# Issuing the first weight quarter and the last row tile's stores from a second engine's DMA queue

## The chip, the cores and the metric

The kernel runs on one core of one Trainium2 chip. The metric is the device time of one execution in microseconds (us). A run also leaves a span (first to last instruction, about 1.7 us shorter than the time) and the mean clock that TensorE was granted, as a share of full speed. Executions are compared on the same chip; those of other chips are only set beside them.

Names: PE is TensorE, PEld its weight loads, DVE VectorE, ACT ScalarE, SP SyncE. SPq and ACTq are the instruction queues of SyncE and ScalarE, from which DMAs are issued. L156 is line 156 of the kernel file; the change adds one line near the top, so L156 of before is L157 of after.

## The reference

The reference mixes two attention blocks over the same input with a gate. Cut to what matters:

```python
x = A_x                                             # [1, 2048, 1024] bf16
g = sigmoid((x * gate_w).sum(-1, keepdims=True))
a = linear_attention(x, A_wqkv, A_wo)               # pq, pk = phi(q), phi(k); 32 heads of 32
b = local_attention(x, B_wqkv, B_wo)                # window 8, dilation 2
return g * a + (1 - g) * b
```

The part that the change touches is the first product of block A: pk = phi(x @ Wk), with x transposed on its way in and Wk of 1024 x 1024.

## The kernel before

All loads go through SyncE's queue, in this order. A "row tile" is 128 rows of x; each is transposed by the DMA (crossbar transpose) into xT. The first half of Wk (512 columns) comes as four quarters, the second half as one load of 1 MB.

```python
WkA = [wpool.tile([P, KT, 512], BF16, name="WkA0", tag="wa")]
nc.sync.dma_start_transpose(out=xT[:, :, 0:P], in_=rows(x, 0, P))
for i in range(4):
    if i == 2:
        nc.sync.dma_start_transpose(out=xT[:, :, P:2 * P], in_=rows(x, P, 2 * P))
    nc.sync.dma_start(out=WkA[0][:, 2 * i:2 * i + 2, :],
                      in_=A_wqkv[2 * i * P:(2 * i + 2) * P, D:D + 512].rearrange("(kt p) n -> p kt n", p=P))
for t in range(2, NB):
    nc.sync.dma_start_transpose(out=xT[:, :, t * P:(t + 1) * P], in_=rows(x, t * P, (t + 1) * P))
WkA += load_w("WkA", A_wqkv, D, "wa", only=(1,))    # the second half of Wk
# ... cut: rows of x, other weights
```

TensorE runs in program order. It starts with 36 small warm-up matmuls, then row tiles 0 and 1 together, as the weight quarters arrive (`kt` 0 to 3 needs quarters 1 and 2), then tiles 2 to 15 for the first half of the columns, then all tiles for the second half.

```python
warm_up(36)
first = [ps_1.tile([P, 512], F32, name="pk_ps", tag="p1") for _ in range(2)]
for t, kts in ((0, (0, 1, 2, 3)), (1, (0, 1, 2, 3)), (0, (4, 5)), (1, (4, 5)), (0, (6, 7)), (1, (6, 7))):
    for kt in kts:
        project(first[t], t, kt, 0)
    # ... cut: phi when a tile is complete
for half in range(2):
    for t in range(NB):
        # ... cut: skips tiles 0 and 1 in half 0
        for kt in range(KT):
            project(pj, t, kt, half)
        phi(pk[:, t, half * 512:(half + 1) * 512], pj)
# ... cut: 350 us of other stages
# in the last stage, for every row tile tb:
nc.scalar.activation(out=osb[:, 0:n], in_=st["ps"][:, 0:n], func=ACT.Copy, scale=omg[:, tb:tb + 1])
nc.sync.dma_start(out=rows(out2, tb * P, (tb + 1) * P)[:, c0:c0 + n], in_=osb[:, 0:n])
```

The softmax here doesn't subtract the row's maximum and nothing guards it: scores larger than these inputs give would overflow.

## Time and profile before

| | before |
|---|---|
| first three runs | 491.37, 491.40, 491.46 us |
| profiled run | 492.63 us: span 490.9 us, mean clock 0.995 |
| PE busy | 484.8 us, 99% of the span |
| unbroken PE work starts | 7.99 us |
| half-clock stretch | 8.41 to 11.82 us (from the clock records) |

The first view is the page of the kernel before: the span, PE's busy time, the granted clock in 40 slices, and the chain that ended last by engine.

```profile
span 490.9 us, 8143 instructions
PE 484.8 (99%) x3332; PEld 230.5 (47%) x3332; DVE 279.1 (57%) x512; ACT 188.4 (38%) x283; POOL 16.0 (3%) x33
...
PEclk8999999999999999999999999999999999999999
...
PE 98%; DMA 1%; SPq 0%; ACT 0%; issue 0%; ACTq 0%
```

PE is the bound, so a few us at the two ends are all that is left outside it. The digit 8 in the first slice (12 us wide) says that PE did not have its full clock there. The clock records begin only at 4.99 us; before that the warm-up matmuls start 0.107 us apart, about twice the 0.056 us of the same matmuls at full clock, so PE had half its clock there too.

The chain that ended last, in order of time, over the first 25 us of before: start, duration, what.

```profile
0.80 1.33 SPq L95
2.13 0.06 issue
2.19 0.57 SPq L99
2.76 0.05 issue
2.81 0.46 SPq L99
3.26 0.04 issue
3.31 4.64 DMA xT<-in_A_x_dram
7.95 0.04 issue
7.99 17.18 PE pk_ps L156 x71
```

SyncE issues one DMA after the other: the first transpose (L95), two weight quarters (L99), the second transpose. PE's unbroken run begins when that transpose has landed. Each issue ahead of it is on the chain, and the first quarter's place is 0.57 + 0.05 us.

The same stretch by windows, before: window, its length, busy time of each engine (and instructions), then the granted clock, the busy share of the DMA engines and GB/s.

```profile
5.00:8.00 3.00, 1.32 (x7) 0.30 (x4) 0.00 (x0) 0.00 (x0) 0.00 (x0) 1.00 1.08 264
8.00:12.00 4.00, 4.00 (x11) 1.51 (x12) 0.00 (x0) 0.00 (x0) 3.16 (x15) 0.57 1.10 252
34.00:36.00 2.00, 2.00 (x11) 0.88 (x9) 1.37 (x3) 0.60 (x1) 0.00 (x0) 1.00 1.05 387
```

From 5 to 8 us PE works 1.32 of 3 us. From 8 to 12 us it is busy all the time but does only about 10 matmuls, where 4 us at full clock hold 18: the clock is 0.57. The DMA engines are busy throughout (shares over 1 are overlapping packets).

### The profile page before, as it was taken

To read this page: it belongs to the slowest core of one execution; us is meant where nothing else is said; L and a number is where in the kernel's file an instruction comes from. 1 tells how busy PE (TensorE), PEld (TensorE's weight loads), DVE (VectorE), ACT (ScalarE), POOL (GpSimd) and SP (SyncE) were. 2 spreads that over 40 slices of the span, in tenths; PEclk is the share of its full clock that TensorE was granted. 3 is DMA by queue.
4 is the path that set the end of the run, shared out by engine and by line. 5 is a ranking of instruction groups with operands and counts; after the bars stand their busy time and mean duration, and the time that the engine had idled before them with its cause. 6 is when DMAs were issued, how large, how long until landed. Compare 5 with 4: busy or idle time off the path is not lost.

```text
span 490.9 us, 8143 instructions
## 1 busy us (share of the span) xinstructions
PE 484.8 (99%) x3332; PEld 230.5 (47%) x3332; DVE 279.1 (57%) x512; ACT 188.4 (38%) x283; POOL 16.0 (3%) x33
## 2 busy tenths in 40 slices
PE   7999999999999999999999999999999999999997
PEld 4444444446444444444445444445545444444444
DVE  0766689993328999997366666656655596000000
ACT  1333311111443333332566665666664332212121
POOL 3000000402000000000000000000000000000000
PEclk8999999999999999999999999999999999999999
DMA  8999960000621222236011151111163953111111
GB/s 193 153 276 371 348 224 0 0 1 5 216 62 61 91 95 88 63 125 196 3 30 37 32 115 30 30 36 29 37 151 81 212 87 85 33 43 33 43 34 43
DMA packets 80181, 46.56 MB, mean 95 GB/s; under 512 B 53520, under 2 KB 74128, under 8 KB 80144
## 3 DMA queue, kind: packets, MB, share of 16 engines
q1 hardware_dynamic: 80144, 46.04, 35.4%
q8 instruction: 26, 0.43, 0.4%
q14 instruction: 11, 0.09, 0.1%
HBM read 21.23 MB, written 7.34 MB: 58 GB/s over the span
## 4 chain that ended last, share of the span: by engine, by line
PE 98%; DMA 1%; SPq 0%; ACT 0%; issue 0%; ACTq 0%
PE kq_ps L331 23%; PE d_ps L444 21%; PE pk_ps L156 11%; PE g_ps L204 11%; PE p_ps L254 11%; PE p_ps L288 8%; PE q_ps L288 3%; PE oB L382 3%; PE s L357 2%; PE q_ps L444 1%; DMA xT<-in_A_x_dram 1%; PE kv_ps L220 1%; PE p_ps L243 1%; SPq L95 0%; SPq L99 0%; ACT osb L449 0%
## 5 line engine op out<-in xcount | busy, mean ns | idle before, releaser
L367 ACT ACTIVATE PT<-s 128x896 bf16<-128x896 f32 (+1 forms) x72 | 63.0, 926 | 24.5 <-PE s L357 24.5
L331 PE MATMUL kq_ps<-xT,WkB 128*128 128x512 bf16 x256 | 65.3, 379 | 0.0
L331 PE MATMUL kq_ps<-xT,WqB 128*128 128x512 bf16 x256 | 64.8, 379 | 0.0
L368 DVE TENSOR_TENSOR PT<-PT,mask 128x896 bf16<-128x896 bf16 (+1 forms) x72 | 44.7, 624 | 26.6 <-ACT PT L367 26.5
L156 PE MATMUL pk_ps<-WkA,xT 128*128 128x512 bf16 x256 | 57.4, 387 | 1.7 <-DMA WkA<-in_A_wqkv_dram 0.9
L254 PE MATMUL p_ps<-WvB,xT 128*128 128x512 bf16 x256 | 58.5, 379 | 0.0
L444 PE MATMUL d_ps<-WoA,pqT 128*128 128x512 bf16 (+1 forms) x248 | 56.9, 372 | 0.0
L444 PE MATMUL d_ps<-WoB,OBT 128*128 128x512 bf16 (+1 forms) x248 | 56.9, 372 | 0.0
L204 PE MATMUL g_ps<-pk,xrow 128*128 128x512 bf16 x256 | 55.4, 379 | 0.0
L144 DVE TENSOR_SCALAR e<-e 128x512 f32<-128x512 f32 x64 | 27.2, 425 | 43.5 <-ACT e L143 43.5
L449 ACT ACTIVATE osb<-d_ps,omg 128x512 bf16<-128x512 f32 (+1 forms) x31 | 20.9, 674 | 76.2 <-PE d_ps L444 76.1
L288 PE MATMUL p_ps<-WqA,xT 128*128 128x512 bf16 x192 | 43.4, 379 | 0.0
L156 PEld LDWEIGHTS <-xT 128*128 128x128 bf16 x256 | 25.5, 100 | 33.5 <-issue 3.5
L336 ACT CAST kqt<-kq_ps 128x512 bf16<-128x512 f32 x48 | 28.2, 588 | 31.8 <-PE kq_ps L331 31.6
L444 PEld LDWEIGHTS <-pqT 128*128 128x128 bf16 x264 | 25.8, 98 | 29.5
L444 PEld LDWEIGHTS <-OBT 128*128 128x128 bf16 x264 | 25.8, 98 | 29.3
L204 PEld LDWEIGHTS <-xrow 128*128 128x128 bf16 x256 | 25.0, 98 | 30.2
L254 PEld LDWEIGHTS <-xT 128*128 128x128 bf16 x256 | 25.0, 98 | 30.0
L288 PEld LDWEIGHTS <-xT 128*128 128x128 bf16 x256 | 24.3, 98 | 28.5
L143 ACT ACTIVATE e<-pk_ps 128x512 f32<-128x512 f32 x32 | 19.0, 597 | 43.8 <-PE pk_ps L156 43.8
L331 PEld LDWEIGHTS <-WqB 128*128 128x128 bf16 x256 | 23.0, 97 | 24.7
L331 PEld LDWEIGHTS <-WkB 128*128 128x128 bf16 x256 | 22.6, 97 | 24.1
(57 smaller groups left out, 400.3 us busy)
## 6 DMA issues: line engine op xcount, KB each, us to landing
xrow<-in_A_x_dram SPq DMA_DIRECT2D x4, 1024.0 KB, 12.7
out_dram<-osb SPq DMA_DIRECT2D x31, 128.0 KB, 1.9
pqd<-tmp SPq DMA_DIRECT2D x12, 256.0 KB, 2.1
WvA<-in_A_wqkv_dram SPq DMA_DIRECT2D x2, 1024.0 KB, 16.6
WoA<-in_A_wo_dram SPq DMA_DIRECT2D x2, 1024.0 KB, 13.7
WvB<-in_B_wqkv_dram SPq DMA_DIRECT2D x2, 1024.0 KB, 11.9
WqA<-in_A_wqkv_dram SPq DMA_DIRECT2D x2, 1024.0 KB, 10.0
WkB<-in_B_wqkv_dram SPq DMA_DIRECT2D x2, 1024.0 KB, 7.4
```

What stands on the lines that cost most here:

```text
L143: nc.scalar.activation(out=e[:], in_=pj[:], func=ACT.Exp)
L144: nc.vector.tensor_scalar(out=e[:], in0=e[:], scalar1=1.0, scalar2=1e-6, op0=ALU.min, op1=ALU.add)
L156: nc.tensor.matmul(pj[:], lhsT=xT[:, kt, t * P:(t + 1) * P], rhs=WkA[half][:, kt, :], start=(kt == 0), stop=(kt == KT - 1))
L204: nc.tensor.matmul(pj[:], lhsT=xrow[:, t, kt * P:(kt + 1) * P], rhs=pk[:, t, half * 512:(half + 1) * 512], start=(t == 0), stop=(t == NB - 1))
L254: nc.tensor.matmul(st["pj"][:], lhsT=xT[:, kt, t * P:(t + 1) * P], rhs=WvB[half][:, kt, :], start=(kt == 0), stop=(kt == KT - 1))
L288: nc.tensor.matmul(st["pj"][:], lhsT=xT[:, kt, t * P:(t + 1) * P], rhs=WqA[half][:, kt, :], start=(kt == 0), stop=(kt == KT - 1))
L331: nc.tensor.matmul(st["pj"][:], lhsT=W[c // 4][:, kt, (c % 4) * P:(c % 4 + 1) * P], rhs=xT[:, kt, cols], start=(kt == 0), stop=(kt == KT - 1))
L336: (nc.vector.tensor_copy if 0 <= after < 4 else nc.scalar.copy)(out=kqt[:, which, cols], in_=st["pj"][:])
L367: nc.scalar.activation(out=ptv[:, hs], in_=s4[:, hs, 0:W_], func=ACT.Exp, scale=SCALE)
L368: nc.vector.tensor_tensor(out=ptv[:, hs], in0=ptv[:, hs], in1=m[:, None, :].broadcast_to([P, 2, W_]), op=ALU.mult)
L444: nc.tensor.matmul(st["ps"][:, 0:n], lhsT=lhsT, rhs=W[c0 // 512][:, c, c0 % 512:c0 % 512 + n], start=(side == 0 and c == 0), stop=(side == ...
L449: nc.scalar.activation(out=osb[:, 0:n], in_=st["ps"][:, 0:n], func=ACT.Copy, scale=omg[:, tb:tb + 1])
```

## The change

The intent: SyncE's queue gives up one slot at the start, so that everything behind it goes out earlier, and the quarter itself leaves beside the first transpose. At the end, ScalarE, which evicts the last results, also stores them, without handing over to SyncE.

```diff
     for i in range(4):
         if i == 2:
             nc.sync.dma_start_transpose(out=xT[:, :, P:2 * P], in_=rows(x, P, 2 * P))
-        nc.sync.dma_start(out=WkA[0][:, 2 * i:2 * i + 2, :],
-                          in_=A_wqkv[2 * i * P:(2 * i + 2) * P, D:D + 512].rearrange("(kt p) n -> p kt n", p=P))
+        (nc.sync if i else nc.scalar).dma_start(
+            out=WkA[0][:, 2 * i:2 * i + 2, :],
+            in_=A_wqkv[2 * i * P:(2 * i + 2) * P, D:D + 512].rearrange("(kt p) n -> p kt n", p=P))
# ... cut
-                    nc.sync.dma_start(out=rows(out2, tb * P, (tb + 1) * P)[:, c0:c0 + n], in_=osb[:, 0:n])
+                    (nc.sync if tb < NB - 1 else nc.scalar).dma_start(
+                        out=rows(out2, tb * P, (tb + 1) * P)[:, c0:c0 + n], in_=osb[:, 0:n])
```

## The prediction

> **What bounds it now.** TensorE. The page gives PE 484.8 us busy of a 490.9 us span (99%), and the chain of waits is 98% PE. The change touches only the two ends.
>
> *Start* (chain of waits and timeline, 0 to 20 us). SyncE issues one after the other: first transpose 0.80, 1.33 us long; weight quarter at 2.19 (0.57 us); second quarter 2.81 (0.46); second transpose 3.31 (1.25), which lands 4.64 us after its start. PE runs 36 warm-up matmuls from 1.12 to 5.13, then waits 0.69 and 0.22 us for the first two weight quarters and 0.76 us for the second transpose. From 7.99 on PE never waits again in this stage.
>
> There is also a clock effect. The records show full clock from 4.99 to 8.41 us, half clock from 8.41 to 11.82 (3.41 us), then full. In that stretch matmuls start every 0.43 us instead of 0.216, so about 1.7 us of PE work is lost. The window before it, 4.99 to 8.41, was about 37% busy (four matmuls and 0.4 us).
>
> *End.* Last matmul ends 487.6; the last eviction takes 0.475 us to 488.18; SyncE issues the last store at 488.21 (0.33 us); it lands about 1.6 us later; the rest is barrier.
>
> **What the change does.** The first quarter's issue leaves SyncE's queue; the order listing puts it on ScalarE directly behind the 1.28 us table load (0.79 to 2.07), with no wait. Every later SyncE issue moves up one slot: 0.57 + 0.05 = about 0.62 us. The second transpose should start near 2.7 and land near 7.3. The quarter itself goes at about 0.9, if the table load does not hold ScalarE's sequencer, or at about 2.1; both are early enough, since PE is in its warm-up until 5 us. So PE's unbroken run starts about 0.6 us sooner, and all 0.6 us is on the chain.
>
> Can later loads keep up? Transposes land at least 1.66 us before PE needs them; the second half of the weights lands 35.88, and is used from 36.45: 0.57 us of slack, and it moves earlier too. So 0.6 us survives; a gain much over 1.2 us would be cut there.
>
> The end: the same hop (0.03 us) and the same issue time, on another engine. Only three stores move, and ScalarE is idle over 1 us before each last eviction, so a 0.33 us issue does not delay it. I expect 0 ± 0.1 us.
>
> **Against the gain.** The Trainium skill, "Perfetto Trace Analysis", DMA Instruction — HWDGE, says that the descriptor generator is locked for exclusive use and that the profiled window includes the wait for that lock. If so, the two issues serialise and the gain is nil. No trace of one queue shows it. "DMA: Bandwidth & Descriptors", Issuing engines are not separate DMA queues, says a second engine saves only the sequencer's issue time: my 0.6 us.
>
> **For more.** If the earlier start makes the 4.99 to 8.41 window busy enough (about 55%), the half-clock stretch could vanish, for up to 0.6 us more before the weight slack binds. I give it one in four.
>
> **Prediction:** 490.8 us, range 489.9 to 491.5. Faster by over 2%: 0.01; within 2%: 0.98; slower: 0.01.
>
> **Right if** the second transpose is issued near 2.7 us and not longer than 1.3 us; the quarter's issue on ScalarE overlaps the first transpose; PE's run starts near 7.4; the span from the last matmul to the end is unchanged at 3.3 us.
>
> **Wrong if** the issues of the two queues lengthen each other; the early quarter delays the first transpose's data; the half-clock window moves or vanishes; or ScalarE's issue is slower and delays the end.

## The result, and the profile after

| | before | after |
|---|---|---|
| median | 491.38 us (6 runs) | 490.98 us (6 runs) |
| lowest to highest | 490.72 to 492.78 | 490.68 to 491.80 |
| profiled run | span 490.9, clock 0.995 | span 489.7, clock 0.999 |

The ratio of after to before is 0.9992, with a 95% interval of 0.9976 to 1.0007. A ratio here is the mean time of one kernel's fast runs over that of the other's of the same rounds, so not quite the ratio of the medians quoted. The two samples overlap, and the first three runs of before, within 0.09 us of each other, had hidden a spread of 2 us.

The page of after:

```profile
span 489.7 us, 8140 instructions
PE 483.1 (99%) x3332; PEld 229.5 (47%) x3332; DVE 279.1 (57%) x512; ACT 188.0 (38%) x283; POOL 16.3 (3%) x33
...
PEclk9999999999999999999999999999999999999999
...
PE 92%; SPq 5%; DMA 2%; issue 0%; ACT 0%
```

The clock digit 8 is gone, PE's busy time is 1.7 us less for the same 3332 matmuls, and the chain now has 5% of SyncE's queue in it. The timeline of after, 0 to 12 us (start, duration, engine, line, operation, what; in brackets the idle time before it and its end), shows the issues and the matmuls:

```profile
0.79 1.28 ACT L70 ACT_TABLE_LOAD   x1 [0.79 <-PEq L495]
...
0.80 1.34 SPq L95 DMA_TRANSPOSE xT<-in_A_x_dram  x1
0.83 0.44 ACTq L99 DMA_DIRECT2D WkA<-in_A_wqkv_dram  x1
...
2.20 0.56 SPq L99 DMA_DIRECT2D WkA<-in_A_wqkv_dram  x1
2.82 1.25 SPq L98 DMA_TRANSPOSE xT<-in_A_x_dram  x1
...
6.13 0.59 PE L157 MATMUL pk_ps<-WkA,xT 128*128 128x512 bf16 x2 [0.87 <-DMA WkA<-in_A_wqkv_dram]
...
7.26 1.04 PE L157 MATMUL pk_ps<-WkA,xT 128*128 128x512 bf16 x4 [0.54 <-DMA xT<-in_A_x_dram]
8.53 3.83 PE L157 MATMUL pk_ps<-WkA,xT 128*128 128x512 bf16 x17 [0.23 <-DMA WkA<-in_A_wqkv_dram]
```

The quarter goes out at 0.83 us, while the table load runs on ScalarE and SyncE issues the transpose. Neither issue is longer than it was on SyncE's queue alone (1.34 against 1.33 us; 0.44 against 0.57). The second transpose is issued at 2.82 in place of 3.31, and tile 1 starts at 7.26 in place of 7.99.

Then come waits that before's profile did not have: one at 8.53 for the third weight quarter, and one near 35 us. The windows of after, and the chain that ended last from 25 to 40 us:

```profile
5.00:8.00 3.00, 1.58 (x8) 0.48 (x6) 0.00 (x0) 0.00 (x0) 0.00 (x0) 1.00 1.12 250
8.00:12.00 4.00, 3.77 (x19) 1.52 (x18) 1.31 (x3) 1.09 (x2) 3.00 (x14) 1.00 1.11 210
34.00:36.00 2.00, 1.48 (x8) 0.51 (x6) 1.36 (x4) 0.60 (x1) 0.00 (x0) 1.00 1.04 399
```

```profile
27.05 8.11 DMA WkA<-in_A_wqkv_dram
35.16 0.05 issue
35.21 4.92 PE pk_ps L157 x22
```

With the full clock, PE reached the second half of Wk before it had landed (35.16 us) and waited 0.68 us: that is where the chain goes over to SyncE's queue. In before, PE came to this point at 36.45, after the landing (35.88).

From there on the two programs are equal. The time from the first matmul of the second half to the last matmul of the kernel is 450.90 us in before and 450.91 in after. So the whole difference of the two spans (1.24 us) is made in the first 36 us: 36.45 against 35.21. The profiles of the experiments below say the same, where their matmul records are complete: the span less the start of the second half is 454.4 or 454.5 us in all of them, and 454.3 where that half comes in four loads (e7, e8, e9).

The end of before, and the end of after:

```profile
487.71 0.47 ACT L449 ACTIVATE osb<-d_ps,omg 128x256 bf16<-128x256 f32 x1 [1.27 <-PE d_ps L444]
488.21 0.33 SPq L451 DMA_DIRECT2D out_dram<-osb  x1
```

```profile
486.43 0.47 ACT L450 ACTIVATE osb<-d_ps,omg 128x256 bf16<-128x256 f32 x1 [1.27 <-PE d_ps L445]
486.93 0.34 ACTq L452 DMA_DIRECT2D out_dram<-osb  x1
```

Eviction start to store issue is 0.50 us in both; from the start of the last matmul to the start of the last instruction it is 3.51 and 3.50 us.

The question left by the result: is the half-clock stretch part of the old start, or did it fall by chance on one profile and not on the other? And how much of 1.24 us comes from the freed slot?

### The profile page after: what moved, and what is told of

It reads as the page before. It is cut to its first block, busy times and chain, and to the rows that moved or that the text cites. A ratio compares the mean times of both kernels' runs of the same rounds, so it can differ in the third digit from the quotient of the medians.

```text
span 489.7 us, 8140 instructions
## 1 busy us (share of the span) xinstructions
PE 483.1 (99%) x3332; PEld 229.5 (47%) x3332; DVE 279.1 (57%) x512; ACT 188.0 (38%) x283; POOL 16.3 (3%) x33
## 4 chain that ended last, share of the span: by engine, by line
PE 92%; SPq 5%; DMA 2%; issue 0%; ACT 0%
PE kq_ps L332 23%; PE d_ps L445 21%; PE g_ps L205 11%; PE p_ps L255 11%; PE p_ps L289 8%; PE pk_ps L157 6%; SPq L103 4%; PE q_ps L289 3%; PE oB L383 3%; PE s L358 2%; DMA WkA<-in_A_wqkv_dram 2%; PE q_ps L445 1%; PE kv_ps L221 1%; PE p_ps L244 1%; SPq L99 0%; SPq L95 0%
## 5 line engine op out<-in xcount | busy, mean ns | idle before, releaser
L157 PE MATMUL pk_ps<-WkA,xT 128*128 128x512 bf16 x256 | 56.2, 379 | 2.2 <-DMA WkA<-in_A_wqkv_dram 1.6
```

Of the source, the lines that this page charges most:

```text
L157: nc.tensor.matmul(pj[:], lhsT=xT[:, kt, t * P:(t + 1) * P], rhs=WkA[half][:, kt, :], start=(kt == 0), stop=(kt == KT - 1))
```

## The experiments

Theory A: the first quarter's move does two things. It frees a slot (earlier transposes), and it makes PE less idle around 5 to 8 us, so that the clock is not halved afterwards. Rival B: the half clock comes by chance with the phase of a free-running window, whatever the kernel, and the gain is that chance. Rival C: the stores carry the gain.

Each experiment has six runs (the profiled one and five timed). Below, spans are sorted and "low" marks a mean clock of 0.997 or less (one stretch of 3.41 us at half clock takes 0.0035 from the mean of a 490 us span). A "long" run is one of 490.0 us span or more. The four kernels of a group ran on one chip, beside 11 runs of the kernel before. The first six runs of the changed kernel, of the result above, had spans of 489.0, 489.0, 489.0, 489.4, 489.7 and 490.1 us, none low.

### Group 1: repeats, and the two halves of the change apart

**b1_before_again** is the kernel before, unchanged.

> The kernel before, unchanged, to see its spread of span and clock run by run. Theory A (the half-clock stretch is part of the old start): most runs show a mean clock near 0.995 and spans near 490.9 us. Rival B (the stretch comes and goes with the phase of the clock window, whatever the kernel): some runs show 0.995 and some 0.999, and those at 0.999 are 0.5 to 0.6 us shorter, not 1.7 us, because the second half of the weights lands at 35.9 us and cuts the rest.

**b1_after_again** is the changed kernel, unchanged.

> The changed kernel, unchanged. Theory A: every run near clock 0.999 or above, spans 489.0 to 490.1 us as in its first six runs, and the spread comes from the landing of the second half of the weights (35.2 us in its first profile), so that the start of the next PE tile follows that landing. Rival B: some runs at 0.995, with spans of 490.2 us or more.

**e1_quarter_only** undoes the second part of the change:

```diff
-                    (nc.sync if tb < NB - 1 else nc.scalar).dma_start(
-                        out=rows(out2, tb * P, (tb + 1) * P)[:, c0:c0 + n], in_=osb[:, 0:n])
+                    nc.sync.dma_start(out=rows(out2, tb * P, (tb + 1) * P)[:, c0:c0 + n], in_=osb[:, 0:n])
```

> Only the first weight quarter moves to ScalarE's queue; all stores stay on SyncE. If the start carries the whole effect: same as the changed kernel within 0.2 us (about 491.0 us, ratio 0.999), second transpose issued near 2.8 us. If the stores carry it: as before, 491.4 us.

**e2_stores_only** is the kernel before with the second part alone:

```diff
-                    nc.sync.dma_start(out=rows(out2, tb * P, (tb + 1) * P)[:, c0:c0 + n], in_=osb[:, 0:n])
+                    (nc.sync if tb < NB - 1 else nc.scalar).dma_start(
+                        out=rows(out2, tb * P, (tb + 1) * P)[:, c0:c0 + n], in_=osb[:, 0:n])
```

> Only the stores of the last row tile move to ScalarE's queue; the quarter stays on SyncE. Expected: no gain, ratio 1.000 within 0.001, and last matmul to end of span 3.50 us as in both profiles (3.51 before, 3.50 after). If the stores carry the effect: 0.4 us faster than before.

Spans of the runs (us):

```
before (11)      488.9 489.0 489.0 489.0 489.1 489.4 | 490.6 490.6low 490.9low 491.0low 491.0low
b1_before_again  489.0 489.1 489.1 489.4 489.4       | 491.4low
e2_stores_only   489.1 489.1 489.1 489.3             | 490.4 491.1low
b1_after_again   488.4 488.6 488.6 488.7 489.1 489.5
e1_quarter_only  488.1 488.6 488.9 489.0 489.0 489.3
```

Ratios to before: 0.9995 (b1_before_again, 0.9974 to 1.0017), 0.9981 (b1_after_again, 0.9962 to 1.0000), 0.9980 (e1_quarter_only, 0.9962 to 0.9999), 1.0000 (e2_stores_only, 0.9976 to 1.0023).

The kernel before has two kinds of runs: around 489.1 us, and around 490.9 us, the latter mostly with a low clock. So the profile that the prediction was made from was of the rarer kind, and theory A as first written for the repeat ("most runs near 0.995") is wrong. Rival B's numbers for before fit better, but not its core: a low clock did not come "whatever the kernel". It came in 6 of 23 runs with the old start and in none of 12 with the quarter on ScalarE. Rival C falls: the stores alone give 1.0000, and the quarter alone gives as much as both. In e2's profile the time from the start of the last matmul to that of the last instruction is again 3.50 us. The repeat of the changed kernel came out shorter than expected (488.4 to 489.5 us).

The profile of b1_before_again, at full clock, is the fair partner of after. Its windows:

```profile
5.00:8.00 3.00, 1.53 (x7) 0.48 (x6) 0.00 (x0) 0.00 (x0) 0.00 (x0) 1.00 1.10 277
8.00:12.00 4.00, 4.00 (x19) 1.60 (x18) 1.18 (x1) 1.08 (x2) 3.51 (x18) 1.00 1.13 228
```

From 8 to 12 us PE works on 19 matmuls at a clock of 1.00, as many as in after: what before's profile lost there was the clock.

At full clock, too, the new start is faster: 488.8 us on average (b1_after_again) against 489.1 in the 11 short runs of before and its repeat (group 3 puts this in doubt).

### Group 2: fill the idle time, keep the slot, move more

**e3_before_fill** lets PE do small matmuls of no use while it waits for the second transpose; no load moves.

```diff
+            warm = ps_1.tile([P, P], F32, name="warm", tag="p1")
             def warm_up(n):
-                warm = ps_1.tile([P, P], F32, name="warm", tag="p1")
# ... cut
             for t, kts in ((0, (0, 1, 2, 3)), (1, (0, 1, 2, 3)), (0, (4, 5)), (1, (4, 5)), (0, (6, 7)), (1, (6, 7))):
+                if t == 1 and kts[0] == 0:
+                    warm_up(16)
                 for kt in kts:
```

> The kernel before with 16 more idle-filling matmuls (about 0.9 us at full clock) where TensorE waits for the second transpose; no load is moved. Theory A (the half-clock stretch follows from too little matmul work in one clock window: 1.3 us of work in the window that was followed by the stretch, about 1.6 us in one that was not): no run with a clock of 0.997 or less, all spans 488.9 to 489.5 us, so faster on average than before by about 0.1 to 0.2% but no faster than the full-clock runs of before. Rival (the stretch is chance, unrelated to that idle time): slow runs of 490.4 to 491.4 us in about a third of the runs, as before.

**e4_slot_kept** puts a tiny load, which nobody reads, into the freed place of the changed kernel.

```diff
+        if i == 0:
+            slot = wpool.tile([P, 2, 16], BF16, name="slot", tag="slot", bufs=1)
+            nc.sync.dma_start(out=slot[:], in_=A_wo[0:2 * P, 0:16].rearrange("(kt p) n -> p kt n", p=P))
         (nc.sync if i else nc.scalar).dma_start(
```

> The changed kernel with a tiny transfer (8 KB, same count of rows) put into the place on SyncE's queue that the first quarter left. Theory A (the gain is the freed issue slot): second transpose issued near 3.3 us again, TensorE's unbroken run starts 0.4 to 0.6 us later than in the changed kernel, full-clock spans back at about 489.1 us. Rival (the gain is the early landing of the first quarter, 3.7 instead of 5.8 us): spans stay at 488.6 us.

**e5_act_all** moves all four quarters.

```diff
-        (nc.sync if i else nc.scalar).dma_start(
+        nc.scalar.dma_start(
```

> All four quarters of the first weight half on ScalarE's queue, SyncE issues only transposes. Slot theory carried on: second transpose issued near 2.2 us, third near 3.5, one more slot each; TensorE's run starts near 6.4 us and the span falls by up to 0.6 us more, to 488.0. If the DMA engines are the limit by now (busy share about 1.1 from 5 to 12 us): transposes land no earlier than in the changed kernel and the span stays within 0.2 us of 488.6.

**e6_after_fill_split** is the changed kernel with 12 filling matmuls (edit as in e3) and the second half of Wk in four loads:

```diff
-    WkA += load_w("WkA", A_wqkv, D, "wa", only=(1,))
+    WkA.append(wpool.tile([P, KT, 512], BF16, name="WkA1", tag="wa"))
+    for i in range(4):
+        nc.sync.dma_start(
+            out=WkA[1][:, 2 * i:2 * i + 2, :],
+            in_=A_wqkv[2 * i * P:(2 * i + 2) * P, D + 512:D + 1024].rearrange("(kt p) n -> p kt n", p=P))
```

> The changed kernel with 12 idle-filling matmuls before the second row tile, and the second weight half loaded in four quarters instead of one load. The fill can only remove slow runs, which the changed kernel did not show in 12 runs; the split removes the 0.68 us wait for the second half where it occurs (seen in one profile of four). Expected: spans 488.4 to 488.8 us, less spread than the changed kernel's 488.4 to 489.5.

Spans (us), on another chip than group 1:

```
before (11)          489.1 489.2 489.3 489.5 489.8 | 490.0 490.6low 490.8 490.8low 490.9low 491.3low
e3_before_fill       489.2 489.2 489.4 489.5       | 490.2 490.5
e4_slot_kept         489.2 489.3 489.4 489.5 489.7 489.9
e5_act_all           489.2 489.3                   | 490.2 490.4 490.8low 490.9low
e6_after_fill_split  488.7 488.7 488.8 488.9 489.1 489.2
```

Ratios: 0.9990 (e3, 0.9972 to 1.0008), 0.9986 (e4, 0.9971 to 1.0001), 0.9999 (e5, 0.9981 to 1.0016), 0.9973 (e6, 0.9959 to 0.9988).

*e3.* No low clock, as theory A expected, but two long runs with a recorded clock of 1.0, which it did not expect. Only half a hit; the next group goes on from here. By length alone (two long runs of six) the fill is not shown to help; the case for it rests on the recorded clock.

*e4.* The timeline of e4_slot_kept shows SyncE's old times again with the quarter still early:

```profile
0.83 0.45 ACTq L102 DMA_DIRECT2D WkA<-in_A_wqkv_dram  x1
...
2.21 0.56 SPq L101 DMA_DIRECT2D slot<-in_A_wo_dram  x1
2.81 0.46 SPq L102 DMA_DIRECT2D WkA<-in_A_wqkv_dram  x1
3.32 1.25 SPq L98 DMA_TRANSPOSE xT<-in_A_x_dram  x1
...
7.29 1.04 PE L160 MATMUL pk_ps<-WkA,xT 128*128 128x512 bf16 x4 [0.25 <-DMA xT<-in_A_x_dram]
8.73 3.55 PE L160 MATMUL pk_ps<-WkA,xT 128*128 128x512 bf16 x14 [0.41 <-DMA WkA<-in_A_wqkv_dram]
```

The span is what the slot theory expected (mean 489.5, as the short runs of before, 489.4), but the way there is not. The second transpose was issued 0.50 us later than in the changed kernel, and tile 1 still started at 7.29, as good as 7.26: from issue to landing it took 3.9 us in place of 4.4 (4.6 in before). So this landing did not hang on the freed slot: with the quarter early, the second transpose lands at 6.87 to 7.46 us in seven profiles, e4's 7.24 among them, and with the old start at 7.54 to 8.01 in six. The slot seems to be lost further on: in e4's profile the third quarter landed at 8.69 us and the third and fifth row tiles at 10.56 and 13.94, against 8.26, 10.25 and 13.77 in e6, which has the changed kernel's issues and ran on the same chip. That is one profile each, and e9's (8.61, 10.35 and 13.98, with the slot free) is close to e4's, so this is not shown. And e4 had no long run. This suggests, without showing it, that two effects come apart: the quarter's early landing (3.73 us) goes with the missing long runs, the freed slot with about 0.4 us at full clock (489.50 on average against 488.90 in e6, of which about 0.15 belongs to e6's end, as told below). Three cautions: the tiny load has 256 rows of 32 bytes to move, so part of this cost may be its own; e6 has a fill and a split besides the slot; and at the old start's rate of low runs, six without one would come by chance once in 9.

*e5.* The timeline and a window of e5_act_all:

```profile
0.83 6.09 ACTq L99 DMA_DIRECT2D WkA<-in_A_wqkv_dram  x4
2.19 1.69 SPq L98 DMA_TRANSPOSE xT<-in_A_x_dram  x1
6.57 1.04 PE L157 MATMUL pk_ps<-WkA,xT 128*128 128x512 bf16 x4 [1.73 <-DMA xT<-in_A_x_dram]
8.14 4.05 PE L157 MATMUL pk_ps<-WkA,xT 128*128 128x512 bf16 x10 [0.53 <-DMA xT<-in_A_x_dram]
```

```profile
8.00:12.00 4.00, 3.81 (x10) 1.46 (x12) 0.00 (x0) 0.00 (x0) 1.68 (x9) 0.60 1.21 240
```

More of the same change loses everything. The second transpose goes out at 2.19 as planned, but with three quarters issued from ScalarE by 2.3 us the *first* transpose lands at 6.52 us, in place of 4.60 with one quarter beside it and 4.21 with none. PE stands idle for 1.73 us, and the half clock is back (0.60), in two runs of six. Neither expected span came (488.0, or within 0.2 us of 488.6): it is 490.1 us on average, as before's. That the transposes land no earlier did come true (the second at 8.09). The Trainium skill, "DMA: Bandwidth & Descriptors", Queues, rings and completion order, says that each DMA engine takes turns between the queues it has work for; the later landing of the transpose agrees with that. (The fourth quarter waited for a completion semaphore, that of the first transpose, and went at 6.54, so this is not a clean test of all four. The second transpose's issue took 1.69 us here in place of 1.25; why is open.)

### Group 3: the two causes of long runs apart

**e7_before_split** is the kernel before with the split of e6 alone.

> The kernel before with the second weight half loaded in four quarters. Two causes of long runs are supposed: (1) a half-clock stretch after a clock window with under about 40% of matmul work (33% and 37% were followed by one, 42% and more were not), (2) a late landing of the second weight half (35.9 us in the first profile; the span is then that landing plus about 454.4 us). The split takes away only cause 2: long runs (490.0 us and more; 14 of 34 so far with the old start) should become fewer but stay, those that stay showing 0.997 or 0.995 where the clock was recorded. If cause 2 were all: none left.

**e8_before_fill_split** is the kernel before with the fill of e3 and the split.

> The kernel before with the 16 filling matmuls and the split, so with both supposed causes of long runs removed and every issue where it was before. Expected: no run of 490.0 us or more, spans 489.0 to 489.6 us. If long runs remain, there is a third cause. What is then left between this and the changed kernel with fill and split (488.7 to 489.2 us) is the freed issue slot: about 0.3 us.

**e9_after_split** is the changed kernel with the split alone.

> The changed kernel with the split alone. If the changed start itself prevents the half-clock stretch (windows of 47% and more in its profiles), the fill of the earlier run was not needed: spans 488.4 to 489.2 us, no run over 489.5. If the fill did it: long runs of 490 us and more.

**e10_after_third** is the changed kernel once more.

> The changed kernel a third time, beside the three others. Expected: no run with a clock of 0.997 or less (none in 12 so far), spans 488.4 to 490.1 us, mean about 1 us below that of before (ratio 0.998), of which about 0.5 us is the earlier start at full clock and the rest is the long runs of before that are missing.

Spans (us), on a third chip:

```
before (11)           489.3 489.3 489.4 489.4 489.4 489.9 | 490.3 490.8low 490.9low 491.1low 491.2low
e7_before_split       488.7 488.7 488.7 489.5             | 490.2 491.2low
e8_before_fill_split  488.9 489.0 489.1 489.6 489.8       | 490.2
e9_after_split        488.3 488.7 488.9 489.0 489.1 489.4
e10_after_third       488.5 488.9 489.0 489.1 489.2 489.3
```

Ratios: 0.9987 (e7, 0.9966 to 1.0007), 0.9986 (e8, 0.9970 to 1.0002), 0.9975 (e9, 0.9959 to 0.9991), 0.9979 (e10, 0.9963 to 0.9996).

Over all groups, runs with a low clock: 14 of 45 with the old start (before, its repeat, e2), all of them 490.6 us or longer; 0 of 24 with the new one (the changed kernel three times, and e1), and 0 of 18 more where the new start was edited further (e4, e6, e9). e5, which sends three quarters early, is not among them: two of its six are low. If the true rate were 14 in 45, 24 runs without one would have a chance of (31/45)^24, about 1 in 7,700; an exact test that leaves the rate open gives about 1 in 930. The fill in the old start gave 0 of 12 (e3, e8), with a chance of about 1 in 90 (1 in 46 by the exact test). The split alone left one in six. By length alone, without the clock records, it is 19 long runs of 45 against 1 of 24.

e8's expectation, no long run, failed by one run of 490.2 us at a recorded clock of 1.0. Five of the old start's 45 runs are of this kind, one of e7's, three of the 12 with fill, one of the changed kernel's 18. Their cause is not settled. A late landing of the second half of Wk was the supposed one, but the split does not remove them. The clock record does not exclude a missed half-clock stretch: e6's profile has no clock record at all, and its mean clock is then given as 1.0, though its matmuls started 0.43 us apart at 4.93 and 5.36 us.

The split also tests the gain at full clock, and there it does not hold: e7's four short runs, with the old start, average 488.90 us, and so do e9's six with the new one. Against e8's five short runs, with the old start, fill and split, e9 is 0.38 us shorter. So how much the new start is worth at full clock, and by which way, stays open.

### What the profiles say of the clock

The clock records of the profiles lie on windows of 3.413 us, at another offset from the kernel's start in each. For the first window that began at full clock I added up the matmul work in it (each matmul counted as its spacing when back to back: 0.21 us for 512 columns, 0.05 for the small ones) and looked at the window behind it:

| profile | matmul work in the window | next window |
|---|---|---|
| e5_act_all | 33% | half clock |
| before | 37% | half clock |
| b1_before_again | 42% | full |
| after, e9_after_split | 47%, 47% | full |
| e7_before_split | 52% | full |
| e3_before_fill | 58% | full |
| e4, e10, b1_after_again, e2, e1, e8 | 64, 68, 69, 72, 77, 98% | full |

So in these profiles the line lies between 37% and 42%; below it there are only two. The old start runs close to it: PE is idle for about 2.1 us of the window in before (0.8 before the first quarter, 0.39 and 0.92 us after it, by the gaps between matmul starts). Whether a run falls below depends on where the window lies and when the second transpose lands. The new start has its first quarter before the warm-up ends, loses the first of these gaps, and stayed above in every profile. Its margin is not large in all of them: by the matmul starts of after, a window from 5.1 to 8.5 us would have held 38% (my estimate: six matmuls of 0.215 us), so another offset could have brought it down to the line. The Trainium skill, "TensorE: Matmul & The Clock Gate", Part 1, tells of such a free-running window of 3413 ns; the records agree, to the digit.

## Why the prediction was right or wrong

The time was predicted as 490.8 us (489.9 to 491.5) and measured as 490.98. Two of the prediction's own "wrong if" points came true all the same: the half-clock window vanished, and the early quarter delayed the first transpose (4.60 against 4.21 us), which cost nothing because PE was in its warm-up until then. Point by point:

- **The two issues do not serialise: right.** The 0.44 us from 0.83 on ScalarE lie within the 1.34 us from 0.80 on SyncE, and neither grew. The table load did not hold the issue either.
- **The second transpose near 2.7 us, not longer than 1.3; PE's run near 7.4: right as numbers.** 2.82, 1.25, 7.26. But the run from 7.26 is not unbroken (the wait at 8.53), and e4 reaches 7.29 with the slot taken again. So the step from the freed slot to the earlier landing is not what these numbers show.
- **The end unchanged: right.** 3.51 and 3.50 us from the last matmul's start to the last instruction's; the stores alone give a ratio of 1.0000.
- **"All 0.6 us is on the chain" and "so 0.6 us survives": too much.** At full clock in both, the changed kernel's runs are 0.3 us shorter than before's short runs on the chip of group 1 (488.8 against 489.1) and 0.45 us on that of group 3 (489.00 against 489.45); with the split in both (e7, e9) they are not shorter at all. The slack of at least 1.66 us that I gave the later transposes was read from a profile in which PE had lost 1.7 us to the half clock. At full clock that slack is used up: in b1_before_again PE already waits 0.12 and 0.19 us for the third and the fifth row tile, and in after 0.40 us for the third quarter (by the gaps between matmul starts). The DMA engines' share is 1.13 and 1.11 from 8 to 12 us there, so I take them, more than SyncE's issue, to set the pace; e4 and e5 point the same way, but no run isolates it.
- **The half-clock stretch as a fixed part of before, to vanish with one chance in four: wrong in kind.** It is in about a third of before's runs (14 of 45), and in none of 42 with the new start (e5 left out). My estimate of 55% matmul work in that window after the change (37% and 0.6 of 3.41 us more) was 47% by the profile.
- **The cap at about 1.2 us by the second half of Wk: right** in the profile of after, which gained 1.24 us and waited 0.68 us there. It is not the rule: in the two repeats of after PE did not wait for it.

The mean effect puts the two parts together. On the chip of group 1 the 17 runs of before average 489.76 us, the six of b1_after_again 488.82: 0.94 us, of which 0.31 is between runs at full clock and 0.63 is long runs that are missing. On the chip of group 3 it is 1.09 us, 0.45 and 0.64. The part of the missing long runs is the better founded of the two. That the prediction came out close to the first measured median is partly luck: before's median falls on its short runs or between the two kinds, depending on how many of six are long.

The version with the split (e9, 0.9975) and that with fill and split (e6, 0.9973) are the fastest against before, but not clearly faster than the changed kernel (0.9979 and 0.9981). About 0.15 us of their spans comes from the end, where the split shifted which semaphore the last store uses: SyncE waits for the semaphores one after the other, about 0.06 us each, and now has fewer left behind the last landing (3.33 us from the last matmul's start, against 3.50).

## What to carry to other kernels

Before moving a load to a second queue, look whether the DMA engines have room at that moment. Here one quarter early, while they were idle (share 0.00 in the first 2 us of before), helped; three of them delayed the transpose that PE needed first. Before reading slack from a profile, look at the clock, and at whether the profiled run took as long as the timed ones (492.63 against 491.4 us here): waits hidden behind a slow stretch come back when it goes. And where a kernel has two kinds of runs, one profile and three equal times show only one of them; list span and clock of many runs before giving a change 0.1%.

## What the Trainium skill lacked or had wrong

- "TensorE: Matmul & The Clock Gate", Why this matters for your kernels, asks for no idle gap over about 3 us. Here the clock was halved after gaps of at most 0.92 us (before, between matmul starts) and 1.73 us (e5_act_all, by the timeline), so keeping to that is not enough: a window of 3.413 us with 33% or 37% of matmul work was enough, 42% kept the clock. The page gives no such share.
- The same page, Part 1, does not say what share of work releases the clock: here windows with 37%, 58% and 62% of (half-clock) matmul work did not release it (e10_after_third, e8, e4), 75% did (e2).
- "Perfetto Trace Analysis", DMA Instruction — HWDGE, says that the descriptor generator is locked for exclusive use and that the wait counts as the instruction's time. Two overlapping issues from SyncE (1.34 us) and ScalarE (0.44 us) were no longer than alone, so no such wait shows here. In e5_act_all three issues from ScalarE (0.44 to 0.49 us each) lie beside SyncE's first two, and the first took 1.33 us as ever; that the second took 1.69 in place of 1.25 is not explained.
- "DMA: Bandwidth & Descriptors", Issuing engines are not separate DMA queues, says that DMAs of all engines interleave on the same DMA engines and that a second one only saves issue time. It does not say that the order of landing changes, which can cost more than the issue saves: the first transpose landed at 4.60 us with one load beside it and at 6.52 with three, against 4.21 with none.
- No page found says whether a DMA issue on ScalarE waits for a table load ahead of it: it did not (0.83 us, inside 0.79 to 2.07).
